# Linear attention and a cosine-gated MLP on one core: q through DRAM in blocks of 32, transposed on VectorE, from batch 2 on

## The chip, the core and the metric

The kernel runs on one core of a Trainium2 chip. TensorE (PE) multiplies matrices into PSUM, VectorE (DVE) and ScalarE (ACT) do the elementwise work, GpSimd (POOL) the reductions over partitions, and SyncE (SP) issues all DMAs, in the order of its program. Each engine runs its own instructions in order and waits on semaphores for the others. The metric is the time of one execution on the device in microseconds; lower is better.

## The reference

q, k and v are float32 of 8 batches, 8 heads, 576 positions and 64 columns. q gets a softmax over its columns, k a softmax over its positions; the two products with v make x, of 4608 rows and 512 columns. x then goes through an MLP whose gate is h cos(h).

```python
q_s = softmax of q over the last axis
k_s = softmax of k over axis 2
kv = np.einsum('bhsd,bhse->bhde', k_s, v)
attn_out = np.einsum('bhsd,bhde->bhse', q_s, kv)
x = np.ascontiguousarray(attn_out.transpose(0, 2, 1, 3)).reshape(B * S, H * D)
h = x @ w_in                 # 512 -> 2048
g = h * np.cos(h)
return (g @ w_out).astype(np.float32)   # 2048 -> 512
```

## The kernel before

**Tiling.** Two heads make a pair; a batch has four pairs (p = 0 to 3), each with 128 columns on the partitions of TensorE. Of the 576 positions of a batch, 512 are its own token tile. The 64 left over of each of the eight batches are put into a DRAM tensor x_left and make a ninth tile, which is done last. The MLP goes over units: a unit is one tile and one of 16 blocks f of 128 columns of w_in. Its first product (unit1, L814) makes h in PSUM; then come turns (ACT, L820), rest (DVE, L824), cos (ACT, L830), gate (DVE, L836), hi (ACT, L840), lo (DVE, L844), and the second product (unit2, L883) into four accumulators. From unit 6 on, a product is three passes with operands split into a high and a low part in float32r, 12 matmuls for each of the two products. Batches 0 and 1 take the first eight blocks, then the other eight, with partial sums in DRAM; later batches take all 16.

**Attention of one batch** (attend, L949). For each pair k and v are loaded; k gets its maximum, its exponential and, on PE, the product kv (L555). q is loaded for two pairs into one tile of 9 x 128 columns (load_q, L457 and L461) and gets its softmax in place: q_max (L621), q_sub, q_exp, q_sum, q_inv and q_norm (L640). Then x_steps (L649) does one pair:

- q_tr (L659): PE transposes four 128 x 128 tiles of q into a PSUM bank (L663); for an even pair a fifth one (L667), which holds the left-over 64 positions of both pairs of the tile, into a second bank. q_side (L673) copies the odd pair's part of that to a tile ql on ACT.
- q_hi and q_lo (L686, L696): the high part of the transposed q on ACT, the low part on DVE, in two pieces (512 and 64 columns). In batches 0 and 1 (XF = 2) q_f32 (L691) copies it whole instead.
- x_mm (L708): the product with kv, in two halves of 288 columns; x_hi and x_lo (L722, L736) split x into the ring x4k; the left-over columns go to a tile xl (L725), and SP stores that tile in x_left (put, L728).

**Buffers.** Each tag has a ring of places (BUFS, L282). kq has two, shared by the tiles of k and of q. PSUM has 2 banks for h, 4 for the accumulators and 2 (att) for kv, q's transposes and x. xl has one, stage (the rows of out) two.

**Order.** Nothing is issued at once. Each step goes into a planner (class Plan) with its engine, an estimated time, what it reads and writes, and a due time; a DMA is a step of SP (0.65 us each) and a step of a modelled bus. The planner simulates the engines with these estimates in several rounds and issues the steps in the order of their simulated starts, so every engine has a fixed order. CFG (L26) has the parameters: the due times (t0, unit, att0, att1, att), the sequence of the first loads (seq), kappa and alpha, FN (blocks from FN on have w_in and w_out converted together) and early (how many of the first units issue their first product in four steps, L846).

Of the kernel before, what the change touches and what calls it, by code (L numbers as in the profile page):

```python
# [11 lines left out]
F32 = mybir.dt.float32  # L12
# [13 lines left out]
CFG = dict(  # L26
    FH=8,
    XF=2,
    PELO=1,
    early=2,  # L30
    F2=6,
    FN=9,
    tags0=("att", "h", "acc"),


    t0=31.73,
    unit=5.38,
    att0=dict(k=(-0.27, 5.55), kv=(13.12, 1.43), q=(3.76, 4.59), qt=(5.86, 3.66), x=(4.46, -1.23)),
    att1=(4.02, 6.3),
    att=dict(k=(1.46, 0.06), kv=(2.52, -1.8), q=(5.25, -0.38), qt=(17.73, 5.03), x=(4.19, 3.79)),  # L40

    seq=[
        ("q", 0), ("q", 1), ("k", 0), ("i", 0), ("k", 1), ("v", 0), ("q", 2),
        ("q", 3), ("k", 2), ("v", 1), ("k", 3), ("v", 2), ("v", 3), ("o", 0),
    ],
    wwin=28.78,

    kappa=1.21,
    rounds=8,
    tables=0,  # L50
    alpha=1.26,
)


# [135 lines left out]
def linear_attention_then_cos_gated_mlp(  # L190
# [18 lines left out]
    nc = tc.nc  # L209
    B, H, S, D = q.shape  # L210
    DM = H * D
    DFF = w_in.shape[1]
    P = 128
    NP = H // 2
    CM = S // P
    NM = CM * P
    NL = S - NM
    NC = CM + 1
# [14 lines left out]
    dr = ctx.enter_context(tc.tile_pool(name="dr", bufs=1, space=bass.MemoryType.DRAM))  # L233
# [27 lines left out]
    def v_frame(t):  # L261
# [11 lines left out]
    w_in = w_in.bitcast(U32)  # L273
    w_out = w_out.bitcast(U32)
    x_left = dr.tile([KC, P, TB], F32, name="x_left")
    part = dr.tile([2, NJ, P, DM], F32, name="part")

    plan = Plan()
    plan.add("POOL", 9.0, None)
    T = {}  # L280
    nth = {}
    BUFS = dict(  # L282
        x4k=8, kq=2, qm=1, qs=2, ql=1, mt=1, m1=1, m=2, r=2, kvt=1, kvw=4, xl=1, stage=2, wc=1, r2=3, ghi=2,
        glo=2, h=2, acc=4, att=2,
    )

    def ring(tag):

        i = nth.get(tag, 0)
        nth[tag] = i + 1  # L290
        return (tag, i % BUFS[tag])

    def quarters(place):
        return [(place, i) for i in range(4)]

    SMALL = ("xl", "ql", "qm", "qs", "r")

    def sbt(shape, dt, tag, name, bufs=None):
        pool = small if tag in SMALL else sb
        return pool.tile(shape, dt, tag=tag, name=name, bufs=bufs or BUFS[tag])  # L300


    for tag, size in (
        ("xl", NL), ("ql", NL), ("qm", 18), ("qs", 18), ("r", 1),
        *((f"w{w}{f}", 2 * DM) for f in range(CFG["FN"]) for w in "io"),
        *((f"w{f}", 4 * DM) for f in range(CFG["FN"], NF)),
        ("x4k", 2 * TB), ("r2", TB), ("ghi", TB), ("glo", TB), ("stage", TB), ("wc", 2 * DM),
        ("kvw", 2 * P), ("mt", 4 * P), ("m1", 2 * P), ("m", 2 * P), ("kvt", P), ("kq", 4 * NC * D), ("qt0", S), ("qt1", S),
    ):
        for i in range(BUFS.get(tag, 1)):  # L310
            sbt([P, size], F32, tag, f"place_{tag}_{i}", BUFS.get(tag, 1))
# [9 lines left out]

    F2, FN = CFG["F2"], CFG["FN"]
    splits = {}
# [9 lines left out]
    def spot(ws, f):  # L333
        return f"w{f}" if f >= FN else f"w{ws}{f}"

    def load_w(w, f, after=0.0, seq=()):
        def load():
            if ("raw", w, f) not in T:
                ws = w if f < FN else "io"
                a = sbt([P, len(ws), DM, 2], U32, spot(ws, f), f"raw_{ws}{f}", 1)  # L340
# [308 lines left out]
    def x_steps(b, p, place, kvw, tq, tx, due_q, due_x):  # L649
        odd = p % 2  # L650
        whole = b < CFG["XF"]
        o1 = ring(tq)
        o2 = ring("ql") if odd else ring(tq)
        xo = [ring(tx), ring(tx)]
        xr, xl = quarters(ring("x4k")), ring("xl")
        cols = [slice(0, HALF), slice(HALF, TB)]
# [16 lines left out]
            nc.scalar.copy(t, T["qlp", b, p])  # L673

        def pieces():
            return zip(
                T["qtp", b, p] + ([T["ql", b, p - 1]] if odd else []),
                (slice(0, NM), slice(NM, S)),
            )

        def q_hi():
            T["qt", b, p] = [
                sbt([P, S], F32R, f"qt{n}", f"qt{n}_{b}_{p}", 1) for n in range(2)
            ]
            for a, cs in pieces():
                nc.scalar.copy(T["qt", b, p][0][:, cs], a)  # L686

        def q_f32():
            t = T["qt", b, p] = sbt([P, S], F32, f"qt{p % 2}", f"qt_{b}_{p}", 1)
            for a, cs in pieces():  # L690
                nc.scalar.copy(t[:, cs], a)  # L691

        def q_lo():
            hi, lo = T["qt", b, p]
            for a, cs in pieces():
                nc.vector.tensor_sub(lo[:, cs], a, hi[:, cs].bitcast(F32))  # L696
# [33 lines left out]
        def x_lo(i):  # L730
# [4 lines left out]
            else:  # L735
                nc.vector.tensor_sub(t[:, 1, cs], o, t[:, 0, cs].bitcast(F32))  # L736

        qr = [(place, 0), (place, 1)]
        cold = 2.0 if b == 0 and p < 2 else 1.0
        plan.add(  # L740
            "PE", (0.44 if odd else 0.55) * cold, q_tr, reads=qr, writes=[o1] if odd else [o1, o2],
            due=due_q,
        )
        if not odd:
            plan.add("ACT", 0.23, q_side, reads=[o2], writes=[ring("ql")])
        if whole:
            qts = [("qt", p % 2)]
            plan.add("ACT", 0.82, q_f32, reads=[o1, o2], writes=qts)
# [7 lines left out]
        for i, us in ((0, 0.4), (1, 0.58)):  # L756
            plan.add("ACT", us, lambda i=i: x_hi(i), reads=[xo[i]], writes=xr if i == 0 else [xr[2], xl])
            if twice:
                o = ring(tx)
# [3 lines left out]
            else:  # L763
                o = xo[i]
            plan.add(
                "ACT" if twice else "DVE", (0.45, 0.38)[i] - 0.04 * twice, lambda i=i: x_lo(i),
                reads=[o, xr[2 * i]], writes=[xr[2 * i + 1]],
# [98 lines left out]
    acc = {}  # L866
# [82 lines left out]
    def attend(b, s0, tags):  # L949
# [45 lines left out]
        for p in range(NP):  # L995
            xr += x_steps(b, p, qr[p // 2], kvw[p], tq, tx, due("qt", p), due("x", p))
# [4 lines left out]
    def need(w, f, seq=()):  # L1001
        if (w, f) not in loaded:
            loaded.add((w, f))
            u = [n for n, o in enumerate(order) if o[1] == f][0] + (0 if w == "i" else 2)
            load_w(w, f, max(0.0, when(u) - CFG["wwin"]), seq)

    def prepare(w, f):
        need(w, f)
        ws = w if f < FN else "io"
        if ws not in ready.setdefault(f, []):  # L1010
# [8 lines left out]
    for u in range(NU + 2):  # L1019
        if u >= 2:  # L1020
            unit2(u - 2, G.pop(u - 2), when(u + 0.4))
        if u < NU:
            b, f = order[u][:2]
# [49 lines left out]
```

## Time and profile before

| | before |
|---|---|
| median of 3 runs | 903.76 us (902.5 to 904.68) |
| the profiled execution | 902.25 us |
| its span in the profile | 900.5 us |
| granted clock of TensorE, mean | 0.996 |
| DMA packets | 95801, of which 53760 under 512 B |
| DMA bytes | 61.59 MB |

The page of the profile gives the busy time of each engine, and the span in 40 slices with the busy share in tenths. The chain of waits follows the work that ended last back to what released it. A group of instructions is given by its line, engine, operation, names and shapes, with its count, busy time, mean time of one, and the idle time of the engine just before. The queues' own rows (SPq) show the issue of DMAs. Where a stretch of the span is given, its times are from the start of the span.

### The profile page before, as it was taken

What the parts mean: (1) busy time and instruction counts of PE and PEld (TensorE: products, weight loads), DVE (VectorE), ACT (ScalarE), POOL (GpSimd) and SP (SyncE); (2) the same over time, 40 slices, a digit from 0 to 9 for tenths busy, and PEclk for the clock granted to TensorE, in tenths of its full rate; (3) what the DMA queues carried; (4) which work ended last, traced back from release to release, by engine and by line L of the source; (5) the groups of instructions that cost most, each with busy time, mean ns of one, the idle gap of its engine ahead of it and who ended that gap; (6) DMA issues with size and microseconds to landing.
All of it is one profiled execution on the core that took longest, in us unless ns stands there. A gap on an engine that the chain in (4) does not pass through costs nothing.

```text
span 900.5 us, 11798 instructions
## 1 busy us (share of the span) xinstructions
PE 872.3 (97%) x4416; PEld 710.1 (79%) x4416; DVE 544.5 (60%) x926; ACT 492.2 (55%) x851; POOL 31.5 (3%) x61
## 2 busy tenths in 40 slices
PE   3889999999999999999999999999999999999997
PEld 2655887888888888888888888888888888888885
DVE  7789888976855675566645674567543353333332
ACT  4798699556634645356635663556433353334332
POOL 1200100000000000010000000000000000000000
PEclk9999999999999999999999999999999999999999
DMA  8961583224220131113201220031100020001002
GB/s 234 301 186 49 159 250 127 71 69 137 52 72 28 43 93 47 30 29 81 73 2 54 70 64 25 28 81 29 48 2 2 2 94 0 1 1 47 1 0 48
DMA packets 95801, 61.59 MB, mean 68 GB/s; under 512 B 53760, under 2 KB 86528, under 8 KB 95744
## 3 DMA queue, kind: packets, MB, share of 16 engines
q1 hardware_dynamic: 95744, 60.84, 23.0%
q8 instruction: 35, 0.57, 0.3%
q14 instruction: 22, 0.18, 0.1%
HBM read 48.23 MB, written 12.58 MB: 68 GB/s over the span
## 4 chain that ended last, share of the span: by engine, by line
PE 90%; ACT 3%; DMA 3%; SPq 2%; issue 1%; DVE 1%; ACTq 0%
PE h L814 41%; PE acc L883 41%; PE x_False L708 3%; PE kv L555 2%; PE qt L663 1%; DMA raw_i<-in_moe_w_in_dram 1%; DMA v_sb<-in_v_dram 1%; PE acc L876 1%; DMA raw_io<-in_moe_w_out_dram 1%; ACT q L628 1%; SPq L461 0%; PE x_True L708 0%; ACT L628 0%; ACT L830 0%; SPq L483 0%
## 5 line engine op out<-in xcount | busy, mean ns | idle before, releaser
L814 PE MATMUL h<-x,w_i 128*128 128x512 f32 x864 | 211.1, 393 | 0.0
L814 PEld LDWEIGHTS h<-x,w_i 128*128 128x128 f32 x864 | 161.1, 188 | 33.9 <-DVE kt L824 0.2
L824 DVE SCALAR_TENSOR_TENSOR kt<-kt,h 128x512 f32<-128x512 int32 x144 | 98.7, 685 | 145.8 <-ACT kt L820 144.9
L883 PE MATMUL acc<-w_o,ghi 128*128 128x512 f32 x600 | 186.6, 392 | 0.0
L820 ACT ACTIVATE kt<-h 128x512 int32<-128x512 f32 x144 | 86.0, 597 | 177.3 <-PE h L814 177.0
L814 PE MATMUL h<-x,w_io 128*128 128x512 f32 x672 | 162.9, 391 | 0.7 <-DVE kt L836 0.7
L883 PE MATMUL acc<-w_io,ghi 128*128 128x512 f32 x504 | 156.8, 392 | 0.0
L814 PEld LDWEIGHTS h<-x,w_io 128*128 128x128 f32 x672 | 124.9, 188 | 26.8 <-DVE kt L836 1.1
L840 ACT CAST ghi<-kt 128x512 fp32r<-128x512 f32 x138 | 85.6, 620 | 107.7 <-DVE kt L836 84.2
L836 DVE TENSOR_TENSOR kt<-kt,h 128x512 f32<-128x512 f32 x138 | 94.7, 686 | 67.8 <-ACT kt L830 67.2
L844 DVE TENSOR_TENSOR glo<-kt,ghi 128x512 fp32r<-128x512 f32 x138 | 95.6, 693 | 64.8 <-ACT ghi L840 63.9
L830 ACT ACTIVATE kt<-kt 128x512 f32<-128x512 f32 x144 | 91.3, 634 | 70.1 <-DVE kt L824 68.8
L883 PEld LDWEIGHTS acc<-w_o,ghi 128*128 128x128 f32 x600 | 111.2, 188 | 22.4
L883 PE MATMUL acc<-w_o,glo 128*128 128x512 f32 x300 | 116.9, 390 | 0.0
L883 PEld LDWEIGHTS acc<-w_io,ghi 128*128 128x128 f32 x504 | 93.3, 188 | 19.1
L883 PE MATMUL acc<-w_io,glo 128*128 128x512 f32 x252 | 98.2, 390 | 0.0
L883 PEld LDWEIGHTS acc<-w_o,glo 128*128 128x128 f32 x300 | 56.3, 188 | 12.0
L883 PEld LDWEIGHTS acc<-w_io,glo 128*128 128x128 f32 x252 | 47.3, 188 | 10.1
L555 PE MATMUL kv<-v_sb,k 128*64 128x66 f32 (+1 forms) x600 | 23.6, 231 | 17.6 <-ACT k L531 16.0
L555 PEld LDWEIGHTS kv<-v_sb,k 128*64 128x64 f32 x600 | 20.3, 143 | 25.6 <-ACT k L531 16.4
L708 PE MATMUL x_False<-qt,kvw 128*128 128x288 f32 x176 | 34.9, 325 | 2.5 <-DMA raw_i<-in_moe_w_in_dram 2.4
L708 PEld LDWEIGHTS x_False<-qt,kvw 128*128 128x128 f32 x176 | 28.1, 191 | 7.5 <-ACT xl L725 2.8
(101 smaller groups left out, 760.1 us busy)
## 6 DMA issues: line engine op xcount, KB each, us to landing
q<-in_q_dram SPq DMA_DIRECT2D x32, 256.0 KB, 3.5
out_dram<-o SPq DMA_DIRECT2D x32, 256.0 KB, 2.4
v_sb<-in_v_dram SPq DMA_DIRECT2D x30, 256.0 KB, 3.3
k<-in_k_dram SPq DMA_DIRECT2D x14, 512.0 KB, 4.0
raw_i<-in_moe_w_in_dram SPq DMA_DIRECT2D x9, 512.0 KB, 5.6
raw_o<-in_moe_w_out_dram SPq DMA_DIRECT2D x9, 512.0 KB, 5.3
raw_io<-in_moe_w_in_dram SPq DMA_DIRECT2D x7, 512.0 KB, 5.6
raw_io<-in_moe_w_out_dram SPq DMA_DIRECT2D x7, 512.0 KB, 6.2
```

The lines of the kernel that those rows point to most:

```text
L555: nc.tensor.matmul(x[h * D : (h + 1) * D, odd : odd + vt.shape[1]], t[:, h, c, :], vt, start=(c == CM), stop=(c == CM - 1),)
L628: nc.scalar.activation(t, t, AF.Exp)
L663: nc.tensor.transpose(a1[:, c * P : (c + 1) * P], t[:, CM * odd + c, :], ident)
L708: nc.tensor.matmul(t[:, 0:HALF], a, c[:, cs], start=(n == 0), stop=(n == len(parts) - 1 and not again))
L814: nc.tensor.matmul(o, a, x, start=(c == 0 and n == 0), stop=(c == KC - 1 and n == 2))
L820: nc.scalar.activation(t, T["h", u], AF.Identity, bias=0.25, scale=1.0 / TWO_PI)
L824: nc.vector.scalar_tensor_tensor(t.bitcast(F32), t, -TWO_PI, T["h", u], op0=ALU.mult, op1=ALU.add)
L830: nc.scalar.activation(t, t, AF.Sin, bias=0.5 * math.pi)
L836: nc.vector.tensor_mul(o, t, T["h", u])
L840: nc.scalar.copy(t, T["kt", u].bitcast(F32))
L844: nc.vector.tensor_sub(t, T["kt", u].bitcast(F32), T["gh", u].bitcast(F32))
L883: nc.tensor.matmul(T["acc", j], a[:, js], w, start=(first and n == 0), stop=(last and n == 2))
```

## The change

From batch 2 on (QD = 2) PE doesn't transpose q. In x_steps three new steps take the place of q_tr and q_side:

- q_out: SP stores the pair's normalised q in one of two DRAM buffers q_rows, one row of 128 columns for each position (two DMAs).
- q_in: SP reads it back into a tile qb in four DMAs. Each of them brings 32 of the 128 columns to 32 partitions: the piece of 32 columns (128 bytes) of position 32 n + k lands in partition 32 g + k at place n. So the 32 x 32 blocks stand where they belong in the transposed matrix, and only within a block rows and columns are exchanged.
- q_blocks: one DVE transpose of 128 x 576, which transposes each 32 x 32 block, into a tile qf.

q_hi and q_lo read qf, in one piece of 576 columns. The tiles qb and qf have one buffer each. The ring of xl gets four buffers in place of one. FN goes from 9 to 8, early from 2 to 1. The sequence of the first loads, the due times, kappa and alpha have other values, so all steps are ordered anew. A scratch area for descriptors of GpSimd's DMAs, of which the kernel issues none, is halved.

```diff
-    early=2,
+    early=1,
     F2=6,
-    FN=9,
+    FN=8,
+    QD=2,
...
-    t0=31.73,
-    unit=5.38,
-    att0=dict(k=(-0.27, 5.55), kv=(13.12, 1.43), q=(3.76, 4.59), qt=(5.86, 3.66), x=(4.46, -1.23)),
-    att1=(4.02, 6.3),
-    att=dict(k=(1.46, 0.06), kv=(2.52, -1.8), q=(5.25, -0.38), qt=(17.73, 5.03), x=(4.19, 3.79)),
+    t0=33.71,
+    unit=5.32,
+    att0=dict(k=(-11.28, 5.44), kv=(18.78, -0.31), q=(5.83, 11.45), qt=(12.05, 4.95), x=(9.45, -8.71)),
+    att1=(5.98, 6.97),
+    att=dict(k=(0.32, 0.1), kv=(3.88, 1.0), q=(5.03, -0.91), qt=(22.82, 6.17), x=(4.44, 4.38)),
     seq=[
-        ("q", 0), ("q", 1), ("k", 0), ("i", 0), ("k", 1), ("v", 0), ("q", 2),
-        ("q", 3), ("k", 2), ("v", 1), ("k", 3), ("v", 2), ("v", 3), ("o", 0),
+        ("q", 1), ("q", 0), ("k", 0), ("i", 0), ("k", 1), ("q", 3), ("q", 2),
+        ("v", 0), ("k", 3), ("v", 1), ("k", 2), ("v", 3), ("v", 2), ("o", 0),
     ],
-    kappa=1.21,
+    kappa=1.36,
-    alpha=1.26,
+    alpha=1.33,
...
+    q_rows = dr.tile([2, S, P], F32, name="q_rows")
...
-        x4k=8, kq=2, qm=1, qs=2, ql=1, mt=1, m1=1, m=2, r=2, kvt=1, kvw=4, xl=1, stage=2, wc=1, r2=3, ghi=2,
-        glo=2, h=2, acc=4, att=2,
+        x4k=8, kq=2, qm=1, qs=2, ql=1, mt=1, m1=1, m=2, r=2, kvt=1, kvw=4, xl=4, stage=2, wc=1, r2=3, ghi=2,
+        glo=2, h=2, acc=4, att=2, qb=1, qf=1, qd=2,
...
+        def q_out():
+            t, r = T["q", b, p // 2], q_rows[p % 2]
+            nc.sync.dma_start(
+                r[0:NM].rearrange("(c t) e -> t c e", t=P), t[:, CM * odd : CM * (odd + 1), :]
+            )
+            nc.sync.dma_start(r[NM:S], t[NL * odd : NL * (odd + 1), 2 * CM, :])
+
+        def q_in():
+            t = T["qb", b, p] = sbt([P, S], F32, "qb", f"qb_{b}_{p}")
+            for g in range(4):
+                nc.sync.dma_start(
+                    t[32 * g : 32 * g + 32].rearrange("k (n i) -> k n i", i=32),
+                    q_rows[p % 2].rearrange("(n k) (g i) -> g k n i", k=32, i=32)[g],
+                )
+
+        def q_blocks():
+            t = T["qf", b, p] = sbt([P, S], F32, "qf", f"qf_{b}_{p}")
+            nc.vector.transpose(t, T["qb", b, p])
+            T["qtp", b, p] = [t]
...
+        if blocks:
+            qd, qb, qf = ring("qd"), ring("qb"), ring("qf")
+            o1 = o2 = qf
+            plan.load(1.1, q_out, reads=qr, writes=[qd], parts=2, due=due_q)
+            plan.load(2.3, q_in, reads=[qd], writes=[qb], parts=4)
+            plan.add("DVE", 0.75, q_blocks, reads=[qb], writes=[qf])
+        else:
+            plan.add(
+                "PE", (0.44 if odd else 0.55) * cold, q_tr, reads=qr, writes=[o1] if odd else [o1, o2],
+                due=due_q,
+            )
+            if not odd:
+                plan.add("ACT", 0.23, q_side, reads=[o2], writes=[ring("ql")])
```

More of the change, by code (lines that the diff above doesn't have):

```diff
@@ L294, in quarters @@
         return [(place, i) for i in range(4)]
-    SMALL = ("xl", "ql", "qm", "qs", "r")
+    SMALL = ("pad", "ql", "qm", "qs", "r")
     def sbt(shape, dt, tag, name, bufs=None):
@@ L303, in linear_attention_then_cos_gated_mlp @@
     for tag, size in (
-        ("xl", NL), ("ql", NL), ("qm", 18), ("qs", 18), ("r", 1),
+        ("pad", NL), ("ql", NL), ("qm", 18), ("qs", 18), ("r", 1),
         *((f"w{w}{f}", 2 * DM) for f in range(CFG["FN"]) for w in "io"),
@@ L307, in linear_attention_then_cos_gated_mlp @@
         ("x4k", 2 * TB), ("r2", TB), ("ghi", TB), ("glo", TB), ("stage", TB), ("wc", 2 * DM),
-        ("kvw", 2 * P), ("mt", 4 * P), ("m1", 2 * P), ("m", 2 * P), ("kvt", P), ("kq", 4 * NC * D), ("qt0", S), ("qt1", S),
+        ("kvw", 2 * P), ("mt", 4 * P), ("m1", 2 * P), ("m", 2 * P), ("kvt", P), ("xl", NL), ("kq", 4 * NC * D), ("qt0", S), ("qt1", S), ("qb", S), ("qf", S),
     ):
@@ L651, in x_steps @@
         whole = b < CFG["XF"]
-        o1 = ring(tq)
-        o2 = ring("ql") if odd else ring(tq)
+        blocks = b >= CFG["QD"]
+        if not blocks:
+            o1 = ring(tq)
+            o2 = ring("ql") if odd else ring(tq)
         xo = [ring(tx), ring(tx)]
@@ L675, in pieces @@
         def pieces():
+            if blocks:
+                return [(T["qf", b, p], slice(0, S))]
             return zip(
@@ L736, in x_lo @@
                 nc.vector.tensor_sub(t[:, 1, cs], o, t[:, 0, cs].bitcast(F32))
+        def q_out():
[15 more added lines that the diff above has]
+            T["qtp", b, p] = [t]
         qr = [(place, 0), (place, 1)]
         cold = 2.0 if b == 0 and p < 2 else 1.0
[L740 to L745, printed above, removed]
+        if blocks:
+            qd, qb, qf = ring("qd"), ring("qb"), ring("qf")
[10 more added lines that the diff above has]
+                plan.add("ACT", 0.23, q_side, reads=[o2], writes=[ring("ql")])
         if whole:
@@ L1051 @@
     from concourse.bass_utils import run_bass_kernel_spmd as _run
-    nc = _bacc.Bacc("TRN2", target_bir_lowering=False, num_devices=1, dynamic_dma_scratch_size=8192)
+    nc = _bacc.Bacc("TRN2", target_bir_lowering=False, num_devices=1, dynamic_dma_scratch_size=4096)
     arrays, args = {}, []
```

## The prediction

> **What bounds the kernel now.** First the page: its line of busy times, and its slices of the span.
>
> ```profile
> PE 872.3 (97%) x4416; PEld 710.1 (79%) x4416; DVE 544.5 (60%) x926; ACT 492.2 (55%) x851; POOL 31.5 (3%) x61
> PE   3889999999999999999999999999999999999997
> PEclk9999999999999999999999999999999999999999
> ```
>
> TensorE (PE) is busy for 97% of the span at full granted clock; only the first three slices and the last are lighter. Since a busy PE is not yet a PE that bounds, the table by stage comes next (stretch, its us, busy us and instructions of PE, PEld, DVE, ACT, POOL, clock, DMA share, GB/s).
>
> ```profile
> 0.00:50.00 50.00, 28.96 (x234) 21.78 (x235) 37.68 (x97) 32.42 (x71) 9.80 (x25) 0.97 0.89 261
> 50.00:80.00 30.00, 29.85 (x120) 18.58 (x117) 25.96 (x41) 29.73 (x55) 0.31 (x1) 1.00 0.45 130
> 127.50:223.41 95.91, 95.22 (x520) 78.21 (x518) 78.91 (x125) 66.23 (x108) 3.80 (x6) 1.00 0.38 118
> 319.40:415.39 95.99, 95.99 (x508) 79.39 (x507) 58.09 (x101) 52.68 (x90) 3.39 (x6) 1.00 0.18 50
> 607.36:727.00 119.64, 119.64 (x563) 99.25 (x563) 60.56 (x98) 54.49 (x99) 0.00 (x0) 1.00 0.07 21
> ```
>
> One batch takes 95.99 us, PE has no gap in it, DVE works 58.09 us and ACT 52.68. In the head it is otherwise: DMA is 0.89 busy up to 50 us, and ACT has 29.73 of the 30 us to 80. The chain of waits says the same of a batch: it is PE from end to end, and its pieces (start, us, what) show where the transposes of q stand.
>
> ```profile
> 353.26 2.72 PE acc L883 x12
> 355.98 0.44 PE qt L663 x4
> 356.42 0.11 PE qt L667
> 356.53 2.76 PE h L814 x12
> ...
> 376.44 0.44 PE qt L663 x4
> 376.88 2.77 PE acc L883 x12
> ```
>
> Twelve matmuls take 2.72 us, but 2.76 or 2.77 behind transposes. So an even pair's five transposes cost 0.44 + 0.11 + 0.04 = 0.59 us of PE, an odd pair's four cost 0.44 + 0.05 = 0.49.
>
> **The change, part by part.**
>
> *PE.* Batches 2 to 7 have 12 even and 12 odd pairs; all their transposes go and nothing comes to PE: 12 x (0.59 + 0.49) = **-12.96 us**, or 2.16 of each batch of 95.99. All of it lies in stages where PE is full (95.22 of 95.91 in batch 2, 119.64 of 119.64 in the last one), so it counts in full unless something else becomes late.
>
> *DVE and ACT.* (line, operation, shape, count | busy, mean ns)
>
> ```profile
> L824 DVE SCALAR_TENSOR_TENSOR kt<-kt,h 128x512 f32<-128x512 int32 x144 | 98.7, 685 | 145.8 <-ACT kt L820 144.9
> L640 DVE TENSOR_TENSOR q<-q,qs 128x1152 f32<-128x1152 f32 x16 | 21.7, 1355 | 0.4
> L696 DVE TENSOR_TENSOR qt<-qt,qt 128x512 fp32r<-128x512 f32 x24 | 16.5, 686 | 10.2 <-ACT qt L686 10.2
> L696 DVE TENSOR_TENSOR qt<-ql,qt 128x64 fp32r<-128x64 f32 x12 | 2.6, 215 | 0.0
> L840 ACT CAST ghi<-kt 128x512 fp32r<-128x512 f32 x138 | 85.6, 620 | 107.7 <-DVE kt L836 84.2 <-PE acc L883 19.5 <-DVE qs L636 4.0
> L686 ACT CAST qt<-qt 128x512 fp32r<-128x512 f32 x24 | 14.0, 583 | 4.5 <-PE qt L663 4.4
> L673 ACT COPY ql<-qt 128x64 f32<-128x64 f32 x16 | 3.6, 223 | 1.1 <-DVE qt L696 1.1
> ```
>
> No row shows a transpose on DVE. By the rows of 512 and 1152 columns a column costs (1355 - 685) / 640 = 1.05 ns, so 576 columns 0.75 us; the bounds are the rows 0.69 and 1.36, and I take 0.75. q_lo becomes one operation of 0.75 in place of 0.69 + 0.22. DVE gains 0.75 - 0.16 = 0.59 us a pair, 2.4 a batch: 60.5 of some 94. On ACT q_hi becomes one cast of about 0.68 in place of 0.58 and a small one, and twelve copies L673 of 0.22 go; ACT gets lighter. Both count nothing: DVE's idle 38 us a batch cover it. Without that cover it would be 24 x 0.75 = 18 us.
>
> *DMA.* Packets are priced from two stretches, one with two loads of q (2304 packets of 256 B, and the rest of a load of v), one with four stores of out (512 of 2 KB):
>
> ```profile
> 331.00:335.00 4.00, 4.00 (x20) 3.30 (x19) 3.37 (x10) 2.35 (x5) 0.00 (x0) 1.00 0.75 173
> 345.00:351.00 6.00, 6.00 (x28) 4.99 (x27) 3.45 (x6) 3.50 (x7) 0.00 (x0) 1.00 0.45 175
> q<-in_q_dram SPq DMA_DIRECT2D x32, 256.0 KB, 3.5
> out_dram<-o SPq DMA_DIRECT2D x32, 256.0 KB, 2.4
> 329.98 0.62 SPq L457 DMA_DIRECT2D q<-in_q_dram  x1
> 330.64 0.70 SPq L461 DMA_DIRECT2D q<-in_q_dram  x1
> ```
>
> 0.75 x 4 x 16 / 2304 = 20.8 ns for 256 B; 0.45 x 6 x 16 / 512 = 84 ns for 2 KB. The line through both gives 16 ns for 128 B and 30 for 512 B. q_out writes 576 packets of 512 B: 576 x 30 / 16 = 1.1 us. q_in reads 4 x 576 packets of 128 B: 2304 x 16 / 16 = 2.3 us, at most 3.0 by the row of 256 B, and, the other way, up to 12 at the 84 ns of the other row; I take 2.3 to 3.0. Four pairs make 14 to 16 us of a batch, on top of a share of 0.18, so about 0.35. SP issues six DMAs more a pair: 24 x 0.65 = 15.6 us a batch on a queue that issues 28 a batch today (4 of k, 8 of q, 8 of v, 4 of out, 4 of x_left), about 18 us.
>
> The Trainium skill, "DMA: Bandwidth & Descriptors" (Specifications), asks for at least 512 B a transfer for line rate and says that below it the engine reads, modifies and writes. By it 128 B should cost no less than 512 B, which would make q_in 2304 x 30 / 16 = 4.3 us, an estimate, and leave the sum as it is (the point from which q comes late is 5.5 us of data, rival C). The trace shows 256 B at a quarter of 2 KB, so no such step.
>
> *The path of q.* From the end of the normalisation: two issues and landing 0.6 + 2.4 = 3.0 to 3.5, four issues 1.9 to the last and its landing 2.4 to 3.5, then 0.75 + 0.68 + 0.75 and three handovers: about 11 us. How long is there?
>
> ```profile
> L640 DVE TENSOR_TENSOR q<-q,qs x2: 1358/1359/1360, 329.1 to 343.1; 128x1152 f32<-128x1152 f32 x2
> L708 PE MATMUL x_False<-qt,kvw x24: 292/295/302, 361.8 to 404.6; 128*128 128x288 f32 x24
> ```
>
> q is normalised by 330.5 (pairs 0, 1) and 344.5 (pairs 2, 3), x begins at 361.8: 31 us for the first pair, so the path fits. Both ends of this cost: nothing, or the rivals below.
>
> *Four buffers for xl* (head of the kernel; an entry in brackets is the idle time before).
>
> ```profile
> 31.94 0.21 ACT L725 COPY xl<-x_False 128x64 f32<-128x64 f32 x1 [3.27 <-DMA x_left<-xl]
> 32.20 0.75 PE L708 MATMUL x_False<-qt,kvw 128*128 128x288 f32 x2 [2.45 <-DMA raw_i<-in_moe_w_in_dram]
> 47.19 0.80 PE L555 MATMUL kv<-v_sb,k 128*64 128x66 f32 x20 [1.20 <-ACT k L531]
> ```
>
> With one buffer ACT waited 3.27 us for a store that stood behind weights, and PE 2.45. That wait goes; what is late next is ACT's exponential of k, for which PE waits again at 47.19. Between -2.45 and 0: I take **-1.2**.
>
> *The new order of the head.* v of pair 0 is loaded behind q of pairs 3 and 2, four issues later: 4 x 0.65 = 2.6. Today it is issued at 6.82 and 7.48, and PE's first kv waits until 14.77 for ACT:
>
> ```profile
> 6.82 0.62 SPq L479 DMA_DIRECT2D v_sb<-in_v_dram  x1
> 14.77 1.35 PE L555 MATMUL kv<-v_sb,k 128*64 128x66 f32 x20 [14.77 <-ACT k L531]
> ```
>
> Part of it is covered: 0 to +2.6, I take **+1.3**. Unit 1 issued whole instead of in four parts: covered by PE's wait at 47.19, nothing, at most three parts of 0.68. Weights 8 converted together: fewer, longer operations where PE is full, nothing. The other due times move everything a little; the order they give I can't see, so +-3 us.
>
> **Sum.** -12.96 - 1.2 + 1.3 = -12.9. The profiled execution took 902.25 us (span 900.5), so 889.4; it is 1.5 below the median of 903.76. Against the median: **891.0 us**.
>
> **The rivals.**
>
> *A, the head gives it back.* ACT is full from 50 to 80 us, so whatever the new order adds there (a wait, a reload of the exponential's or the sine's table) delays everything behind it. For it: due times, sequence and conversions all change. Against: the work itself is the same. 5 us more is 896, 12 us more is no change. Chance 0.14 (0.08 still faster, 0.06 within 0.2%).
>
> *B, SP stands behind q_out (slower).* q_in waits on SP until q_out has landed, and what is queued behind it waits too: rows of out, loads of v and k. The place is the end of a batch:
>
> ```profile
> 344.43 4.10 SPq L930 DMA_DIRECT2D out_dram<-o  x4
> 347.10 1.07 ACT L922 COPY o<-acc 128x512 f32<-128x512 f32 x2
> 347.65 0.62 PE L883 MATMUL acc<-w_o,ghi 128*128 128x512 f32 x2
> ```
>
> Two staging buffers serve four rows of out, so ACT's third copy starts as soon as the first store has landed (344.43 + 2.4), and the next batch's third group needs that bank about 1.3 us after it is copied. If a wait of 3.1 and four issues of 0.65 stand ahead of the stores, PE loses 3.1 + 2.6 - 1.3 = 4.4 us, in six batches 26: 917 us. It decides from 12.9 / 6 = 2.2 us a batch. Against: the normalisation ends at 344.5, and the first pairs could be through by then. Chance 0.08.
>
> *C, short pieces are dear (slower).* DVE executes in order, so q_blocks waiting for q_in holds up the units' own DVE steps, and PE with them:
>
> ```profile
> 363.38 0.69 DVE L844 TENSOR_TENSOR glo<-kt,ghi 128x512 fp32r<-128x512 f32 x1
> 365.85 0.39 PE L883 MATMUL acc<-w_o,glo 128*128 128x512 f32 x1
> DVE qm L621 <- DMA q<-in_q_dram: 7.8, 9, 1.6
> ```
>
> A unit's last DVE step ends 1.8 us before PE takes it, and waits of DVE for q of up to 1.6 us pass today without a gap in PE. The planner counts 6.1 us from the first issue of q_in to its use (4 x 0.65, 0.2, 2.3, 1.0), so late means over 7.9. With 2.4 for the landing, 5.5 us remain for 2304 packets: 38 ns each. At 50 ns a pair comes 1.7 us too late, 24 of them 41 us: 932. It turns slower at 42 ns. Chance 0.08. The far end, 0.01 of these: if q_in took 19 times the 1.1 us of the same bytes in 512 B, 21 us, a pair would be 15 us late, 24 of them 370 us, about 1260 us; runs of 128 B stay whole here, and the row of 256 B at 20.8 ns speaks against it. That factor is the Trainium skill's, the same page (Rules for kernel authors), for a transpose by a plain DMA with a rearranged access pattern against the hardware's.
>
> **Numbers.** Forecast 0.70 (886 to 897 by the bounds of the head), A 0.14, B 0.08, C 0.08. Faster 0.70 + 0.08 = 0.78, within 0.2% (902.0 to 905.6, about what a measurement of this kernel can tell from no change) 0.06, slower 0.16. For 8 in 10 the range takes the forecast and the part of A that stays faster: 885.5 to 902.
>
> **What would show it.** Right: a batch of about 93.8 us with PE full; no L663 after batch 1; DVE's transposes near 0.75 us; a DMA share near 0.35; no wait of ACT for x_left. B would show as PE or ACT waiting at L922 for stores of out, C as DVE waiting for qb over 2 us with gaps in PE, A as a batch 2 that begins later than before. Wrong would be a batch that stays at 96 us, or a q_in that lands after more than 8 us.

## The result, and the profile after

| | before | after |
|---|---|---|
| median | 903.72 us (902.5 to 904.68, 4 runs) | 889.21 us (889.1 to 890.12, 4 runs) |
| the profiled execution | 902.25 us | 889.29 us |
| its span | 900.5 us | 887.5 us |

The ratio after to before is 0.9842, with a 95% interval of 0.9825 to 0.9859: the change saves 14.5 us. The two profiled executions are 12.96 us apart, since the one of before lies 1.5 below its median; that this is the very number of the prediction's PE term is chance.

The page of the changed kernel, its line of busy times and the DMA queue's line (packets, MB, share of the 16 engines' span):

```profile
PE 858.2 (97%) x4308; PEld 699.4 (79%) x4308; DVE 554.1 (62%) x923; ACT 487.9 (55%) x812; POOL 30.4 (3%) x61
q1 hardware_dynamic: 167168, 75.00, 31.2%
```

The queue's line before:

```profile
q1 hardware_dynamic: 95744, 60.84, 23.0%
```

PE has 108 matmuls less, the transposes of batches 2 to 7, and is as full as before. DVE has 9.6 us more, ACT 4.3 less, the DMA queue 71424 packets more. The stages of the changed kernel, with the columns of the prediction's table:

```profile
50.00:80.00 30.00, 30.00 (x122) 19.11 (x121) 25.42 (x43) 29.52 (x55) 0.31 (x1) 0.96 0.44 129
127.50:227.41 99.91, 98.64 (x522) 80.30 (x521) 81.23 (x127) 66.88 (x101) 3.40 (x6) 1.00 0.44 119
320.90:414.37 93.47, 93.47 (x489) 77.60 (x489) 59.57 (x102) 52.08 (x84) 3.39 (x6) 1.00 0.31 77
```

A batch takes 93.47 us in place of 95.99, and PE still has no gap in it. Where in the span was the time won? Counting the work that is left answers it without matching stages by hand: the matmuls of the first product (h) from a moment to the end (stretch, us, busy us and count, clock, DMA share, GB/s). Before:

```profile
150.00:900.50 750.50, 365.32 (x1512) 1.00 0.15 44
717.41:900.50 183.09, 91.90 (x384) 0.99 0.08 24
```

After:

```profile
150.00:887.50 737.50, 364.08 (x1512) 1.00 0.25 64
704.31:887.50 183.19, 91.91 (x384) 0.99 0.08 24
```

Both kernels have 1512 of them left at 150 us. With 384 left, the changed kernel is 13.1 us earlier, and behind that both need the same 183 us. So head and tail gave nothing by this count, and the batches from 2 on gave all of it.

The chain of waits of one batch, after:

```profile
342.89 1.32 PE kv L557 x40
344.21 2.95 PE acc L917 x12
...
358.04 0.79 PE x_False L714 x6
358.83 2.76 PE h L848 x12
...
413.05 1.32 PE kv L557 x40
```

and a part of it before, which the prediction didn't look at:

```profile
318.67 0.73 PE kv L555 x20
319.40 2.96 PE acc L883 x12
...
327.80 0.73 PE kv L555 x20
328.54 2.96 PE h L814 x12
```

The transposes are gone from the chain. But a second thing has changed: before, a batch's four products kv stood in three groups (a group of 40 and two of 20), after, in two groups of 40. Behind each group the next twelve matmuls take 2.95 or 2.96 us in place of 2.72, and two groups of 20 take 1.46 where one of 40 takes 1.32. One group less is 0.23 + 0.14 = 0.37 us. Transposes 2.16 + kv 0.37 = 2.53, and 95.99 - 93.47 is 2.52. This holds for the steady batches and can't be taken six times: counted over the whole trace, the head and batch 2 have two groups of kv more than before, so that 24 groups became 21, not 19.

The new path of q, first the operations on DVE and ACT (count | busy, mean ns), then the DMAs (KB, us to landing), then one read of four DMAs as SP issues it:

```profile
L762 DVE STREAM_TRANSPOSE qf<-qb 128x576 f32<-128x576 f32 x24 | 18.5, 771 | 0.0
L702 DVE TENSOR_TENSOR qt<-qf,qt 128x576 fp32r<-128x576 f32 x24 | 18.0, 750 | 1.1 <-ACT qt L692 1.1
L692 ACT CAST qt<-qf 128x576 fp32r<-128x576 f32 x24 | 16.1, 671 | 0.7 <-PE x_False L714 0.4
qb<-q_rows SPq DMA_DIRECT2D x96, 72.0 KB, 2.5
q_rows<-q SPq DMA_DIRECT2D x24, 256.0 KB, 2.4
341.08 2.09 SPq L755 DMA_DIRECT2D qb<-q_rows  x4
```

The idle time ahead of the transposes is 0.0: DVE never waited for qb. From the first issue to the last landing a read takes about 2.1 + 2.5 = 4.6 us, an estimate from one issue and the median landing.

### The profile page after: what moved, and what is told of

Read it like the earlier page. It is cut to its first block, busy times and chain, and to the rows that moved or that the text cites. A ratio compares the mean times of both kernels' runs of the same rounds, so it can differ in the third digit from the quotient of the medians.

```text
span 887.5 us, 11706 instructions
## 1 busy us (share of the span) xinstructions
PE 858.2 (97%) x4308; PEld 699.4 (79%) x4308; DVE 554.1 (62%) x923; ACT 487.9 (55%) x812; POOL 30.4 (3%) x61
## 4 chain that ended last, share of the span: by engine, by line
PE 91%; DMA 3%; SPq 2%; ACT 2%; DVE 1%; issue 1%; ACTq 0%
PE h L848 43%; PE acc L917 41%; PE x_False L714 3%; PE acc L910 2%; PE kv L557 2%; DMA v_sb<-in_v_dram 1%; DMA raw_io<-in_moe_w_out_dram 1%; DMA k<-in_k_dram 1%; SPq L463 1%; SPq L459 0%; ACT L864 0%; PE qt L667 0%; ACT raw_io L374 0%; DVE kt L870 0%; SPq L485 0%
## 5 line engine op out<-in xcount | busy, mean ns | idle before, releaser
L848 PE MATMUL h<-x,w_i 128*128 128x512 f32 x768 | 188.0, 394 | 0.3 <-ACT x L740 0.3
L848 PE MATMUL h<-x,w_io 128*128 128x512 f32 x768 | 185.4, 390 | 1.2 <-DVE kt L870 1.2
L917 PE MATMUL acc<-w_io,ghi 128*128 128x512 f32 x576 | 178.2, 390 | 0.0
L848 PEld LDWEIGHTS h<-x,w_i 128*128 128x128 f32 x768 | 144.4, 189 | 31.5 <-ACT x L740 0.7
L848 PEld LDWEIGHTS h<-x,w_io 128*128 128x128 f32 x768 | 143.1, 188 | 31.3 <-DVE kt L870 2.0
L917 PE MATMUL acc<-w_o,ghi 128*128 128x512 f32 x528 | 163.7, 391 | 0.0
L917 PEld LDWEIGHTS acc<-w_io,ghi 128*128 128x128 f32 x576 | 107.2, 188 | 22.5 <-ACT o L956 0.7
L917 PE MATMUL acc<-w_io,glo 128*128 128x512 f32 x288 | 112.1, 389 | 0.0
L917 PE MATMUL acc<-w_o,glo 128*128 128x512 f32 x264 | 102.8, 389 | 0.0
L917 PEld LDWEIGHTS acc<-w_o,glo 128*128 128x128 f32 x264 | 49.6, 188 | 10.4
L557 PE MATMUL kv<-v_sb,k 128*64 128x66 f32 (+1 forms) x600 | 22.8, 231 | 16.4 <-DMA v_sb<-in_v_dram 14.1
L728 ACT CAST x<-x_False 128x288 fp32r<-128x288 f32 x64 | 23.7, 370 | 18.2 <-PE x_False L714 18.1
```

The costliest lines, as they stand in the source:

```text
L557: nc.tensor.matmul(x[h * D : (h + 1) * D, odd : odd + vt.shape[1]], t[:, h, c, :], vt, start=(c == CM), stop=(c == CM - 1),)
L728: nc.scalar.copy(T["x", b, p][:, 0, cs], o[:, 0 : cs.stop - cs.start])
L848: nc.tensor.matmul(o, a, x, start=(c == 0 and n == 0), stop=(c == KC - 1 and n == 2))
L917: nc.tensor.matmul(T["acc", j], a[:, js], w, start=(first and n == 0), stop=(last and n == 2))
```

## The experiments

Theory: PE is full, and what it no longer does comes off the time; DMA, DVE and the longer path are hidden. Rivals: the new order makes the gain; the four buffers of xl make it; the new path has little room and was near to costing. Each run was timed beside the kernel before on the same chip; the ratios are to that, and runs are compared by them, since medians were taken on different chips.

**q back on PE, in the order of the change.** In the changed kernel:

```diff
-    QD=2,
+    QD=9,
```

> The changed kernel with its order parameters, its four xl buffers and FN = 8, but with PE transposing q in every batch (QD = 9), so that the planner orders it anew. Theory (the gain is PE time taken off a full PE): 13 us come back, so 902 us, at least 899, and a batch near 95.6 to 96.0 us. Rival (the gain is the new order, the due times and the buffers): it stays within 3 us of the changed kernel, 889 to 892.

Measured: 901.56 us, ratio 0.997 (0.9958 to 0.9981). The chain of this run:

```profile
335.61 1.32 PE kv L557 x40
...
355.03 0.44 PE qt L667 x4
355.47 0.11 PE qt L671
...
431.24 1.32 PE kv L557 x40
```

The transposes stand in the chain again, and a batch is 431.24 - 335.61 = 95.63 us, 2.16 more than in the changed kernel: the term of the prediction, to the hundredth. Of the gain of 1.58% only 0.3% is left, some 2.7 us; 1.28%, 11.6 us, went with the transposes. The remainder is what order, buffers and FN bring without DRAM, and kv stands in two groups here too, 0.36 us less a batch than before.

**q through DRAM, in the order of before.** In the changed kernel, all order parameters of before:

```diff
-    early=1,
+    early=2,
-    FN=8,
+    FN=9,
...
-    t0=33.71,
-    unit=5.32,
+    t0=31.73,
+    unit=5.38,
```

(and att0, att1, att, seq, kappa and alpha likewise)

> The changed kernel, q through DRAM and four xl buffers kept, but with the order parameters of before (due times, sequence of the first loads, kappa, alpha, FN = 9, early = 2). Theory: the PE time is gone all the same, so 889 to 892 us; a batch of 93.8 us if kv stands in three groups as before, 93.5 if in two. Rival (the order makes the gain): 899 us or more. Second rival (DRAM's longer path fits only with the new due times): gaps in PE of 1 us or more for x in each batch, 895 to 905.

Measured: 892.94 us, ratio 0.9877 (0.9859 to 0.9895). Its chain has kv in three groups, and a batch takes 406.08 - 312.21 = 93.87 us:

```profile
312.21 1.32 PE kv L557 x40
319.20 0.73 PE kv L557 x20
328.33 0.73 PE kv L557 x20
...
406.08 1.32 PE kv L557 x40
```

The time lies 1 us above what the theory allowed and far from the rival: with the old order 1.23% of the 1.58% are there. The batch is as the theory has it; 0.40 us of each batch and some waits in the head are the order's part. The second rival falls too: the batch shown has no gap in PE, and all of PE's waits of 1 us and more end before 300 us.

**The transposes put back on PE, no step moved.** In the changed kernel, ahead of a pair's first x matmul, into the bank which that matmul overwrites:

```diff
+            if blocks and i == 0:
+                for c in range(CM if odd else CM + 1):
+                    nc.tensor.transpose(t[:, 0:P], ident, ident)
             for n, (a, c) in enumerate(parts):
```

> The changed kernel in its own order, with q through DRAM, and besides four or five transposes of the identity on PE ahead of each pair's first x matmul from batch 2 on, into the bank that this matmul then overwrites. No step of the plan moves. Theory: PE is full, so the 108 transposes cost 12 to 13 us: 901 to 902 us, and 2.0 to 2.2 us more a batch. Rival (PE has slack that the page doesn't show): less than 4 us more.

Measured: 901.41 us, ratio 0.9967 (0.9954 to 0.998). The chain of this run (L715 are the added transposes):

```profile
362.06 0.55 PE x_False L715 x5
362.61 0.80 PE x_False L717 x6
...
385.19 0.44 PE x_False L715 x4
385.63 0.80 PE x_False L717 x6
```

4 or 5 transposes take 0.44 or 0.55 us, and the time grows by 0.9967 - 0.9842 = 1.25% of 904, 11.3 us, give or take about 2 by the two intervals. Everything else the same, PE's time alone is worth most of the gain. The trace says why it is a little below 12.96: a batch is 95.44 us (kv at 323.60 to kv at 419.04), 1.97 more than 93.47, which is the transposes' own 2 x (0.55 + 0.44) = 1.98; they stand next to x, and no second stretch of 2.76 us follows them.

**One buffer for xl in the changed kernel** (`xl=4` to `xl=1`):

> The changed kernel with one buffer for xl in place of four; the planner orders it anew. Theory: the buffers are worth 0 to 2.4 us in the head and nothing later, 889 to 891.5 us. Rival (the buffers let the planner put kv in two groups and the stores later): a batch of 93.8 us and more, 891 to 895 us.

Measured: 891.05 us, ratio 0.9852 (0.9834 to 0.9869), kv in two groups, a batch of 93.47 us. The rival falls; the ratios are 0.1% apart, 0.9 us, outside the steady batches, and the intervals overlap.

**Four buffers for xl in the kernel before** (`xl=1` to `xl=4`):

> The kernel before with four buffers for xl and nothing else changed (the ring moved to the other pool, the scratch area halved as in the change). Theory: PE's gap of 2.45 us near 30 us goes, and later waits take part of it: 901.5 to 903.7 us, a batch of 96.0. Rival (the buffers are a good part of the gain): 899 us or less.

Measured: 903.17 us, ratio 0.9991 (0.9979 to 1.0003): no gain that can be told from none. Waits of PE in this run (in total, times, longest):

```profile
PE qt L663 <- ACT qt L691: 2.4, 2, 1.3
PE h L814 <- DVE g L836: 1.7, 1, 1.7
PE qt L663 <- DVE x L736: 1.7, 1, 1.7
PE x_False L708 <- ACT kvw L583: 1.0, 1, 1.0
```

PE's wait of 2.45 us near 30 us is gone, and in the newly planned head others of 1.0 to 1.7 us stand in its place.

**Each DVE transpose twice**, no step moved:

```diff
             nc.vector.transpose(t, T["qb", b, p])
+            nc.vector.transpose(t, T["qb", b, p])
```

> The changed kernel with each transpose on DVE done twice, in its own order: 24 x 0.77 = 18.5 us more of DVE work. Theory (DVE's idle time covers it, steps that wait for DVE have 1.8 us to spare): 0 to 2 us more, 889 to 891 us. Rival (DVE is on the path through the units' steps): 0.77 us a pair shows on PE, 18 us more, 907 us.

Measured: 889.46 us, ratio 0.9833 (0.9816 to 0.9851), DVE busy for 570.2 us in place of 554.1. DVE's work costs nothing here.

**q read back in pieces of 64 bytes**, the plan as it was:

```diff
-                    t[32 * g : 32 * g + 32].rearrange("k (n i) -> k n i", i=32),
-                    q_rows[p % 2].rearrange("(n k) (g i) -> g k n i", k=32, i=32)[g],
+                dst = t[32 * g : 32 * g + 32].rearrange("k (n j i) -> j k n i", j=2, i=16)
+                src = q_rows[p % 2].rearrange("(n k) (g j i) -> g j k n i", k=32, j=2, i=16)
+                for j in range(2):
+                    nc.sync.dma_start(dst[j], src[g, j])
```

> The changed kernel with q read back in pieces of 64 bytes: eight DMAs a pair in place of four, 4608 packets in place of 2304; the plan still counts four DMAs and 2.3 us. It shows how much room the read has. Theory (room of 1.8 us and more before PE notices): q comes 2.5 to 3 us later, most of it hidden, 0 to 6 us more: 889 to 895 us. Rival (the path of q is tight): each of 24 pairs is 2 us late or more, 935 us or more.

Measured: 891.64 us, ratio 0.9861 (0.9847 to 0.9876). DVE's wait for q, which the changed kernel doesn't have:

```profile
DVE qf L762 <- DMA qb<-q_rows: 7.6, 10, 2.1
```

Ten of 24 transposes waited, 7.6 us in all. The ratio rises by 0.19%, 1.7 us, which the intervals alone don't tell from nothing; but in the trace PE waits 3.8 us for DVE's kt and o, where the changed kernel has 1.2, so about 2 us came through.

**In pieces of 32 bytes** (the same with j = 4, i = 8):

> The changed kernel with q read back in pieces of 32 bytes: 16 DMAs and 9216 packets a pair; the plan still counts four DMAs and 2.3 us. Theory (rival C of the prediction as worked out: PE notices from 7.9 us after the first issue): SP issues for 16 x 0.5 = 8 us, the last lands 2.3 us later, so 10.3 us, 2.4 us too late, 24 times: 58 us more, 947 us, at least 925. Rival (most pairs have their q long before PE's order asks for it, as the run with 64 bytes says, where 10 of 24 waited at all): less than 20 us more, under 909.

Measured: 958.83 us, ratio 1.0614 (1.0597 to 1.0631): 6% slower than the kernel before. The read on SP's queue, the wait of DVE, and the waits of PE:

```profile
371.18 9.66 SPq L758 DMA_DIRECT2D qb<-q_rows  x16
DVE qf L762 <- DMA qb<-q_rows: 83.9, 18, 6.6
PE h L848 <- DVE kt L870: 32.9, 11, 6.2
PE acc L917 <- DVE o L953: 13.2, 3, 6.0
PE acc L917 <- DVE glo L878: 5.1, 2, 4.7
```

This is rival C, made to happen. PE doesn't wait for x: DVE stands in front of q_blocks, the units' own steps queue behind it (kt, o, glo), and PE waits for those. What makes it late is, by the trace, SP's issue more than the packets: 16 DMAs in 9.66 us here and in about 8.7 in the median of the reads, while 9216 packets of about 9 ns on 16 engines are 5 us. No run changed the one without the other. And not all of the 70 us are waits. The line of busy times of this run:

```profile
PE 879.1 (92%) x4308; PEld 710.9 (74%) x4308; DVE 552.7 (58%) x923; ACT 486.2 (51%) x812; POOL 30.4 (3%) x61
```

In a span of 958.2 us PE is idle for 79.1, 50 more than in the changed kernel; and the same 4308 matmuls keep it busy for 21 us more, at a mean granted clock of 0.968 in place of 0.997.

**Batch 1 through DRAM as well**, a try at a faster kernel:

```diff
-    QD=2,
+    QD=1,
...
+            if whole:
+                T["qt", b, p] = t
...
-        if whole:
+        if whole and blocks:
+            qts = [qf]
+        elif whole:
```

> The changed kernel with q through DRAM from batch 1 on (QD = 1). Batch 1 multiplies the transposed q as it is, so ACT doesn't copy it (four copies of about 0.83 us and two small ones go), and 18 transposes leave PE. Theory: PE has 2 us less, ACT 3.8 us less in a stage where it is full (29.5 of 30 us between 50 and 80); gain 1 to 4 us, 885 to 888 us. Rival (in the head DMA is 0.9 busy to 50 us, and the longer path of q delays x of batch 1): 889 us or more.

Measured: 892.64 us, ratio 0.9873 (0.9853 to 0.9893): a miss. The stretch from 60 to 80 us, first of the changed kernel:

```profile
60.00:80.00 20.00, 20.00 (x75) 12.46 (x74) 17.55 (x28) 19.62 (x40) 0.31 (x1) 1.00 0.29 76
```

then of this run, and PE's two waits in that stretch:

```profile
60.00:80.00 20.00, 15.42 (x52) 9.06 (x51) 17.22 (x31) 18.39 (x35) 0.42 (x2) 1.00 0.57 144
PE h L852 <- ACT w_i L405: 2.9, 1, 2.9
PE acc L914 <- DVE room L396: 1.7, 1, 1.7
```

ACT is less full, and PE has 4.6 us of gaps where it had none: two conversions of weights, on ACT (w_i) and on DVE (room), come later, while DMA's share has gone from 0.29 to 0.57. The rival has the time right and the place wrong: no DVE transpose of this run waits for qb, so PE's gaps are not waits for q's longer path. **Only pairs 2 and 3 of batch 1** (`blocks = 4 * b + p >= 6`):

> The changed kernel with q through DRAM also for pairs 2 and 3 of batch 1, multiplied there as it is, without ACT's copies; pairs 0 and 1 of batch 1 stay on PE. Theory (the run with all of batch 1 lost its gain because its first pairs' q came late behind a full DMA; the later pairs have more room): 887 to 889 us, PE without waits of over 1.5 us between 50 and 100 us. Rival (in the head every more DMA or a new order of its own costs more than PE's 1 us and ACT's 1.9 us bring): 889.5 us or more.

Measured: 893.3 us, ratio 0.9891 (0.9873 to 0.991): a miss too, with PE busy for 26.14 of the 30 us from 50 to 80, and again no transpose on DVE waits for qb. Whether the DMAs themselves or the order that the planner finds for them do the harm in the head was not told apart. No version faster than the change was found.

## Why the prediction was right

**Sign, size, range.** Forecast were 891.0 us and faster with 0.78; measured 889.21, inside the range. The sum put the gain at 12.9 us; it is 14.5 between the medians and 13.0 between the spans of the two profiles.

**PE, -12.96 us.** Right, in place and size. A batch is 2.16 us longer with the transposes on PE in the same set of parameters (95.63 against 93.47), six times that is 12.96. As whole runs, q back on PE costs 11.6 us and the transposes put back without moving a step 11.3; both have 12.96 within their noise.

**DVE and ACT, nothing.** Right: 0.77 us a transpose against 0.75, DVE at 59.57 us a batch against 60.5, and twice the transposes cost nothing (0.9833 against 0.9842).

**DMA.** Rightly counted as nothing, but priced too high. The queue's time went from 0.230 x 900.5 = 207.1 to 0.312 x 887.5 = 276.9 us of all 16 engines; the difference of 69.8 over 24 pairs is 2.9 us a pair, where the prediction had 3.4 to 4.1 and a share of 0.35 (the profile says 0.31). The DMA records in the traces give the mean time of a packet: 27.7 ns for 512 B, 17.9 for 256 B and 12.8 for 128 B, where the prediction had 30, 20.8 and 16. Its stretch for 256 B held 2432 of those packets and 134 of 512 B, more than the 2304 that it divided by. The Trainium skill's 512 B for line rate ("DMA: Bandwidth & Descriptors", Specifications) is no cliff here: q_in's packets of 128 B did not cost as much as those of 512 B. By bytes they are the slower ones, 10 B a ns against 18.

**The path of q.** Right: DVE never waited for q. The point of rival C, 7.9 us from first issue to use, was a fair bound: with 64 bytes a read took 4.1 to 6.2 us to issue (mostly under 4.5) and 2.3 to land, so most stayed under it and a few went over, and about 2 us came through; with 32 bytes, at some 8.7 + 2.3 = 11.0 us, the rule says 24 x 3.1 = 74, and 70 came. Part of that agreement is luck, since 18 of the 24 transposes waited and 21 of the 70 us are PE's longer busy time. Its cause was put down wrongly: the prediction made it a matter of ns for a packet, and in the runs it was mostly the number of issues on SP.

**Rival A** did not come: with 1344 products of h left, where batch 2's tile begins, the changed kernel stands at 235.68 us in place of 238.07.

**Rival B** did not come. The third and fourth copies of out do wait for the stores, but little (in total, times, longest), and no matmul of PE waits for them:

```profile
ACT o L956 <- DMA out_dram<-o: 3.0, 6, 1.1
```

**The head, -1.2 and +1.3.** The sum of about nothing was right, its two terms were not what happened; that they cancelled was luck. Two rows of PE and one of SP, after:

```profile
10.29 0.62 SPq L481 DMA_DIRECT2D v_sb<-in_v_dram  x1
14.08 1.35 PE L557 MATMUL kv<-v_sb,k 128*64 128x66 f32 x20 [14.08 <-DMA v_sb<-in_v_dram]
19.87 1.12 PE L667 MATMUL qt<-ident,q 128*128 128x128 f32 x4 [3.18 <-ACT qt L697]
```

v is issued 3.5 us later, and now it is v that PE waits for; yet the first kv starts 0.69 us earlier, since the exponential of k, which ended last before, is earlier too. The gap at xl is gone, and PE has one of 3.18 us for ACT's copy of q instead. Both terms priced one wait with everything else left in place, while the planner made a new head. PE is busy for 28.36 of the first 50 us, against 28.96 before.

**What was left out.** The order's own part, which the prediction bounded by +-3 us and took as nothing, is 0.30% without DRAM (q back on PE) and 0.35% with it (the order of before): 2.7 and 3.2 us for the better, known to about 1 and 2 us. Of it, 0.36 to 0.40 us of each steady batch is kv in two groups, which is shown. For the profiled executions the account closes, if each group of kv counts 0.37. PE is busy for 872.3 - 858.2 = 14.1 us less, which is the 12.96 of the transposes and 1.1 of three groups of kv; its idle time grew from 28.2 to 29.3 us; and 14.1 - 1.1 is the 13.0 between the spans. The other 1.5 of the 14.5 us are the distance of the profiled execution of before from its median. The 35 executions of that kernel beside the experiments run from 902.05 to 907.27 us, the two fastest at a granted clock of 0.997 and the two slowest at 0.993 and 0.992; whether this is all of the 1.5 us stays open.

## What to carry to other kernels

Where one engine is full without a gap, count its own instructions and take them off; a path that is several times longer costs nothing as long as it starts early enough and ends in front of an in-order engine that is not made to wait. Find that point by making the path worse on purpose: here twice as many DMAs cost about 2 us, four times as many 70. And the same trick in the head, where PE waits for other work, brought nothing in the two orders tried, so an engine's full share has to be read stage by stage.

## What was not expected of the hardware

- Behind the 64-wide products of kv the next twelve matmuls take 2.95 or 2.96 us in place of 2.72, once for each group, whether it has 20 or 40 products.
- Packets get cheaper below 128 B, but slowly. By the queue's share, q's read and write rose by 1.2 us a pair with 64 B (0.344 x 890.4 us) and by 3.2 with 32 B (0.369 x 958.2 us). With 27.7 ns for each packet of 512 B that q_out writes, this leaves about 13, 11 and 9 ns for packets of 128, 64 and 32 B; the DMA records say 12.8, 10.4 and 8.5. SP's issue, 0.5 to 0.6 us for each DMA, weighed more: 16 DMAs took it about 8.7 us.
- In the run with 32 bytes, where PE is idle for 50 us more, the granted clock is lower, too: 0.968 to 0.973 in its four executions, against 0.996 to 0.999 in the changed kernel's.
